# A merge of two instruction streams planned with traced VectorE times and a ScalarE clock, in a kernel of windowed attention and capacity-routed experts

## Chip, cores and metric

The kernel runs on one core of one Trainium2 chip. The metric is the device time of one execution in microseconds (us); of several runs the median counts. The engines are named as the profile names them: PE (TensorE matmuls), PEld (its weight loads), DVE (VectorE), ACT (ScalarE), POOL (GpSimd) and SP (SyncE).

## What is computed

Attention over a window of 64 positions feeds a layer of eight experts. Each token goes to one expert; an expert takes at most 576 tokens, and tokens are handed out in the order of all 4608 x 8 logits. Cut to what matters:

```python
# attention: batch 8, heads 8, seq 576, head_dim 64, causal window 64
x = attn_out.transpose(0, 2, 1, 3).reshape(4608, 512)
logits = x @ w_gate                       # 4608 x 8
order = np.argsort(-logits.flatten())
for idx in order:                         # greedy, cap = 576 tokens for each expert
    tok, e = idx // 8, idx % 8
    if assigned[tok] >= 0 or counts[e] >= cap: continue
    assigned[tok] = e; counts[e] += 1
for e in range(8):
    h = np.maximum(x[assigned == e] @ w1[e], 0.0)     # 512 -> 1024
    out[assigned == e] = h @ w2[e]                    # 1024 -> 512
```

## The kernel before

The attention comes first (to about 149 us); it also leaves the logits in the tile `L` and the rows of x in DRAM (`xs`). After it, three kinds of work run side by side, all on the same five engines.

**Routing** (`Routing.steps(p)`, p = 0 to 7). Pass p finds the p-th expert that fills up, and its 576 tokens. A pass begins with the choices of each token (six DVE operations, L499 to L506, which end with the tile `one`), goes through eight rounds, and ends with the list of the tokens. A round compares the values with 15 thresholds on DVE (tile `G`, L514), counts on PE (nine matmuls, L593, from here on "a count"), and works out the next thresholds in a chain of small DVE operations (L602 to L654). For p of 1 and more, ACT first spreads `one` fourfold (three copies, L557, into `one4`), which the counts read. The list is made by a sum over positions on PE (L707, L708), one-hot tiles on DVE and ACT (`A`, `B`, `R`, L739 to L748), 18 matmuls (L756), a copy `ils` on DVE (L763) and 8 small matmuls (L768), and ends in the tile `idx` (L774).

**Transposes** (`Experts.turn(p, idx)`). POOL gathers the tokens' rows of `xs` in five indirect DMAs (`xg`, `rest`, L957). PE transposes each tile of 128 tokens (4 matmuls, L975; two PSUM tiles `tp`), ACT rounds it to the high part `xh` (L946), DVE subtracts for the low part `xl` (L950). For p of 1 and more the tiles go as two, two and one.

**Products** (`Experts.steps(p, idx)`). The first product takes 192 matmuls (`h`, L1021), whose results ACT and DVE turn into `hh` and `hl` (L993, L998); the second takes 16 (L1054) and 96 (`o`, L1064), whose results ACT copies (`low`, `ot`, L1038, L1035) and POOL stores by an indirect DMA (L1043). The three terms are xh·wh, xh·wl and xl·wh. `Experts.load` fetches the weights on SP's queue (`st`), ACT makes `wh` (L900) and the negative of it (L911), and POOL's accumulating DMA adds `st` to make `wl` (L913).

Every engine executes in the order in which the program is recorded. That order comes from `Streams.run`: each piece of work is a generator that records instructions and yields a delay in ns, and the generators are resumed in the order of a reckoned clock. `busy(dt, eng)` reckons an engine as a queue: it adds dt to the engine's end and returns how far off that is. Before the change DVE work is entered by `dve(dt)`, which puts 0.4 dt on the queue and 0.6 dt behind it; ACT has no queue, its work is a plain delay. `GATHER`, `JOIN` and others are constants of that clock. For p > 1 a group of transposes waits until the routing has recorded its next matmuls (`self.joins > n0`), or until `JOIN` ns have passed:

```python
    def dve(self, dt):
        return self.busy(0.4 * dt, "dve") + 0.6 * dt
...
                n0, t0 = self.joins, self.clock() + JOIN[tiles[0] // 2]
                yield lambda: self.routed or self.joins > n0 or self.clock() >= t0
```

Below, "expert p" is the expert of pass p, and H_p, O_p are its first and second product.

Of the kernel before, what the change touches and what calls it, by code (L numbers as in the profile page):

```python
# [10 lines left out]
FT = mybir.dt.float32  # L11
FR = mybir.dt.float32r
BF = mybir.dt.bfloat16
# [10 lines left out]
E = 8  # L24
# [374 lines left out]
class Routing:  # L399
# [132 lines left out]
    def dve(self, dt):  # L532

        return self.busy(0.4 * dt, "dve") + 0.6 * dt

    def steps(self, p):
# [7 lines left out]
        if p < E - 1:  # L544
# [19 lines left out]
            for r in range(NR):  # L564
# [4 lines left out]
                if not p:  # L569
# [8 lines left out]
                    yield self.dve(1350)  # L578
                else:
                    c4 = self.room(128, 72)  # L580
                    cn, c4 = c4[:, 64:72], c4[0:M, 0:4 * ND]
                    for j0, j1 in ((0, 20), (20, 36)):
                        self.compare(G, thr, j0, j1)
                        yield self.dve(420)
                    for f in rest:
                        f()
                    yield self.dve(200) + slack
# [18 lines left out]
                    yield self.dve(450)  # L606
# [60 lines left out]
                yield self.dve(400)  # L667
            for f in rest:
                f()
            yield self.dve(200)  # L670
# [11 lines left out]
            yield self.dve(600)  # L682
# [8 lines left out]
            yield self.dve(600)  # L691
        else:
# [7 lines left out]
            yield self.dve(800)  # L700
# [4 lines left out]
        yield self.dve(250) + (600 if p else 0)  # L705
# [7 lines left out]
                                       op0=OP.add, op1=OP.mult)  # L713
        si = tile_([128, 3, NJ], I32, name="si")
        nc.vector.scalar_tensor_tensor(si[:, 0], Y[:, 0], -1.0, Y[:, 1], op0=OP.add, op1=OP.add)
        yield self.dve(500)
# [4 lines left out]
        yield self.dve(500)  # L721
# [18 lines left out]
        yield self.dve(410)  # L740
        nc.scalar.activation(Rw[:, 0], pairs(A_), AF.Copy, scale=self.lane)
        if p:
            nc.vector.tensor_tensor(Bw, pairs(self.r32), sb[:, 1].rearrange("p (q h) -> p q h", h=2)[:, None]
                                    .to_broadcast([128, 32, NJ // 2, 2]), OP.is_equal)
            yield self.dve(1200)
        for j0, j1 in ((0, NJ),) if p else ((0, 18), (18, 36)):
# [5 lines left out]
            yield self.dve(600) + slack + (500 if p else 0)  # L752
# [7 lines left out]
            yield self.busy(n * (18 if p else 29) + (90 if p else 0))  # L760
        yield self.dve(200) + slack
        ils = tile_([72, 32, 2], BF, name="ils")
        nc.vector.tensor_copy(ils.rearrange("p a h -> p (a h)"), il[0:72])  # L763
        yield self.dve(300)
# [7 lines left out]
        yield self.busy(100) + 200 + slack  # L772
# [4 lines left out]
        if p < E - 1:  # L777
            if not p:
                nc.vector.scalar_tensor_tensor(self.eid, m, T[:, 0:1], best, op0=OP.is_gt, op1=OP.mult)
            eq = tile_([128, NJ], FT, name="eq")  # L780
            nc.vector.scalar_tensor_tensor(eq, Y[:, 1], CAP + 0.5, X[:, 1], op0=OP.is_lt, op1=OP.mult)
            nc.vector.scalar_tensor_tensor(self.eid, eq, code[:, 0:1], self.eid, op0=OP.mult, op1=OP.add)
            nc.vector.tensor_scalar(self.un, self.eid, 0.0, None, op0=OP.is_equal)
            yield self.dve(400)
            e1 = tile_([128, E], FT, name="e1")
            nc.vector.tensor_scalar(e1, self.cw, code, -FAR, op0=OP.is_equal, op1=OP.mult)
            nc.vector.tensor_tensor(V, V, e1[:, None, :].to_broadcast([128, NJ, E]), OP.add)
            yield self.dve(600)

            nc.vector.scalar_tensor_tensor(self.oh, m[:, :, None].to_broadcast([128, NJ, E]), T[:, 0:1], one,  # L790
                                           op0=OP.is_gt, op1=OP.mult)
            c2 = tile_([128, E], BF, name="c2")
            with nc.allow_low_precision(reason="whole numbers up to 36"):
                nc.vector.tensor_reduce(c2, self.oh.rearrange("p j e -> p e j"), axis=AX.X, op=OP.add)
            e2 = tile_([128, E], FT, name="e2")
            nc.vector.tensor_scalar(e2, self.cw, code, -1.0e6, op0=OP.is_equal, op1=OP.mult)
            nc.vector.tensor_tensor(self.left, self.left, e2, OP.add)
            if 0 < p < E - 2:
                self.kept = c2
                yield self.dve(1100)  # L800
                return
            yield self.dve(1100) + (slack if p < OWN else 1500)
            cn = self.room(128, E)
            nc.tensor.matmul(cn, self.ones, c2, start=True, stop=True)
            self.joined()
            yield self.busy(110) + 200 + slack
            nc.vector.tensor_tensor(self.left, self.left, cn, OP.add)
            yield self.dve(200)
# [21 lines left out]
class Experts:  # L830
# [34 lines left out]
    def load(self, p, ei):  # L865
# [26 lines left out]
        for i in range(2 * NCH):  # L892
# [8 lines left out]
            yield 1050  # L901
# [7 lines left out]
            else:  # L909

                nc.scalar.activation(lo, hi.bitcast(FT), AF.Copy, scale=-1.0)  # L911
                yield 1150
# [25 lines left out]
    def turn(self, p, idx):  # L938
# [4 lines left out]
        def evac(a, n, t):  # L943
# [4 lines left out]
            yield 700  # L948
# [12 lines left out]
        there = self.clock() + self.busy(6400, "pool") + GATHER[p > 0]  # L961
# [4 lines left out]
        for tiles in ((0, 1), (2, 3), (4,)) if p else ((0,), (1,), (2,), (3,), (4,)):  # L966
            yield max(0, there - 1280 * (4 - tiles[-1]) - self.clock())
            if p > 1:

                n0, t0 = self.joins, self.clock() + JOIN[tiles[0] // 2]  # L970
                yield lambda: self.routed or self.joins > n0 or self.clock() >= t0
            for n, a in enumerate(tiles):
# [3 lines left out]
                dt = self.busy(260)  # L976
# [7 lines left out]
    def steps(self, p, idx):  # L984
# [44 lines left out]
        self.first += 1  # L1029

        def put(a, o):
            ot = fw.tile([128, DM], FT, name="ot", bufs=3)
            m = 128 if a < 4 else 64
            if a < 4:
                nc.scalar.activation(ot, o, AF.Copy)  # L1035
            else:
                t = fw.tile([64, DM], FT, name="low")
                nc.scalar.activation(t, o[64:128], AF.Copy)  # L1038
                yield 650
# [67 lines left out]
def body(tc, q, k, v, vt, wg, w1, w2, xs, out):  # L1107
    nc = tc.nc
    with ExitStack() as ctx:
# [17 lines left out]
        def route():  # L1127
            for p in range(E):
                for dt in rt.steps(p):
# [3 lines left out]
                    if p in rt.idx and p not in listed:  # L1133
                        listed.add(p)
                        st.add(ex.turn(p, rt.idx[p]))
                    yield dt
            ex.routed = True
# [6 lines left out]
        known, listed = set(), set()  # L1144
# [20 lines left out]
```

## Time and profile before

| | |
|---|---|
| median of 3 runs | 650.95 us (649.75 to 651.98) |
| profiled execution | 650.87 us, its span 648.9 us |
| PE busy in the span | 611.3 us (94%) |
| DVE, ACT, POOL busy | 454.1, 346.1, 186.2 us |
| mean granted TensorE clock | 0.972 |

The span runs from the first to the last instruction; 1.97 us lie around it. A row of the timeline gives the start, the duration, engine, line, operation, output and inputs with their shapes, how many instructions were merged, and in brackets how long the engine had been idle and what released it. Matmuls are pipelined, so a matmul's duration overlaps the next one's: the pitch of a run of matmuls is read from their starts. PEclk is the granted TensorE clock, 1.00 for 2.4 GHz and 0.50 for 1.2 GHz.

### The profile page before, as it was taken

The page shows a single profiled execution, that of the slowest core. Times are in us where ns is not written, and L with a number is a line of the kernel's source. Part 1 is how long each engine was busy: PE and PEld are TensorE (multiplying, and loading weights), DVE is VectorE, ACT ScalarE, POOL GpSimd, SP SyncE. Part 2 cuts the span into 40 slices and gives each one's busy share as a digit, 9 for nine tenths or more (in the row PEclk, how much of TensorE's full clock was granted, in tenths as well). Part 3 has the DMA queues.
Part 4 walks back from the last instruction along what each step waited for, and adds up shares of the span by engine and source line. Part 5 has one row for each costly group of instructions (what it writes and reads, how often), then busy time and mean ns, then how long its engine had stood idle before and what let it go on. Part 6 is the DMA issues. An engine that isn't in the chain of part 4 may idle for free.

```text
span 648.9 us, 16904 instructions
## 1 busy us (share of the span) xinstructions
PE 611.3 (94%) x6375; PEld 532.0 (82%) x6375; DVE 454.1 (70%) x2126; ACT 346.1 (53%) x724; POOL 186.2 (29%) x242
## 2 busy tenths in 40 slices
PE   8899999994599999999899999999999999999996
PEld 6677778884389879978797898899789879989985
DVE  7788888886789868876786787688678755523300
ACT  6798999980265176337526643572664354524210
POOL 1334353331141162026105411620541164011011
PEclk9999999996599998999899999999999999999999
DMA  9999999931376199459918964991896399411001
GB/s 313 373 367 368 371 385 368 336 109 36 130 237 130 30 315 240 82 195 218 234 21 300 246 120 149 247 242 30 295 248 122 124 273 321 153 36 38 1 25 48
DMA packets 44657, 127.81 MB, mean 197 GB/s; under 512 B 4632, under 2 KB 5272, under 8 KB 44576
## 3 DMA queue, kind: packets, MB, share of 16 engines
q1 hardware_dynamic: 30736, 79.52, 34.1%
q0 software_dynamic: 13552, 46.69, 30.8%
q8 instruction: 50, 0.82, 0.5%
q10 hardware_dynamic: 288, 0.52, 0.3%
q14 instruction: 31, 0.25, 0.1%
HBM read 82.15 MB, written 18.87 MB: 156 GB/s over the span
## 4 chain that ended last, share of the span: by engine, by line
PE 49%; issue 20%; POOL 4%; DMA 2%; ACT 1%; DVE 0%; POOLq 0%; ACTq 0%
PE h L1021 22%; PE o L1064 18%; PE o L1054 3%; POOL out L1043 2%; PE rps L593 2%; DMA wl<-st 1%; PE tp L975 1%; POOL xg L957 1%; DMA xg<-xs,idx 1%; POOL wl L913 1%; PE rps L756 1%; ACT wh L900 0%; ACT wl L911 0%; PE rps L758 0%; POOLq L1161 0%
## 5 line engine op out<-in xcount | busy, mean ns | idle before, releaser
L1043 POOL DMA_INDIRECT out<-ot,idx x40 | 40.4, 1010 | 252.8 <-ACT ot L1035 87.8
L993 ACT ACTIVATE hh<-h 128x256 fp32r<-128x256 f32 (+1 forms) x128 | 52.4, 409 | 110.3 <-PE h L1021 109.0
L1064 PE MATMUL o<-wh,hh 128*128 128x512 f32 x256 | 101.4, 396 | 0.0
L1064 PE MATMUL o<-wh,hl 128*128 128x512 f32 x256 | 100.8, 394 | 0.0
L1064 PE MATMUL o<-wl,hh 128*128 128x512 f32 x256 | 100.5, 393 | 0.0
L141 ACT ACTIVATE pe<-st,mx 128x128 f32<-128x128 f32 x288 | 92.0, 393 | 5.8 <-DVE mx L136 5.5
L1021 PE MATMUL h<-xh,wh 128*128 128x256 f32 (+1 forms) x512 | 93.0, 302 | 1.7 <-issue 0.9
L1021 PE MATMUL h<-xl,wh 128*128 128x256 f32 (+1 forms) x512 | 93.4, 300 | 0.0
L998 DVE SCALAR_TENSOR_TENSOR hl<-h,hh 128x256 fp32r<-128x256 f32 x128 | 53.6, 419 | 56.5 <-ACT hh L993 55.9
L1021 PE MATMUL h<-xh,wl 128*128 128x256 f32 (+1 forms) x512 | 91.9, 299 | 0.0
L1021 PEld LDWEIGHTS h<-xh,wh 128*128 128x128 f32 x512 | 76.8, 192 | 2.8 <-ACT xh L946 1.4
L1021 PEld LDWEIGHTS h<-xh,wl 128*128 128x128 f32 x512 | 76.7, 192 | 0.0
L1021 PEld LDWEIGHTS h<-xl,wh 128*128 128x128 f32 x512 | 76.6, 192 | 0.0
L900 ACT ACTIVATE wh<-st 128x1024 fp32r<-128x1024 f32 x64 | 67.3, 1052 | 2.7 <-DMA st<-w 2.5
L136 DVE CUSTOM_DVE_ANT_0 st<-Sp,mask 128x128 f32<-128x128 f32 x288 | 63.7, 285 | 5.7 <-PE Sp L128 5.2
L913 POOL DMA_DIRECT2D wl<-st x49 | 44.6, 976 | 68.9 <-ACT wl L911 25.9
L1035 ACT ACTIVATE ot<-o 128x512 f32<-128x512 f32 x32 | 19.1, 597 | 70.9 <-PE o L1064 63.2
L1064 PEld LDWEIGHTS o<-wh,hl 128*128 128x128 f32 x256 | 48.1, 188 | 9.6
L1064 PEld LDWEIGHTS o<-wl,hh 128*128 128x128 f32 x256 | 48.1, 188 | 9.3
L1064 PEld LDWEIGHTS o<-wh,hh 128*128 128x128 f32 x256 | 48.1, 188 | 9.3
L911 ACT ACTIVATE wl<-wh 128x1024 fp32r<-128x1024 f32 x49 | 51.8, 1056 | 0.6
L168 PE MATMUL Op<-VO,pt 128*64 128x73 f32 x640 | 45.3, 230 | 2.5 <-ACT pt L150 1.1
(182 smaller groups left out, 1093.2 us busy)
## 6 DMA issues: line engine op xcount, KB each, us to landing
st<-w SPq DMA_DIRECT2D x60, 512.0 KB
wl<-st POOLq DMA_DIRECT2D x49, 512.0 KB
xs<-x SPq DMA_DIRECT2D x36, 256.0 KB
VO<-v SPq DMA_DIRECT2D x6, 1168.0 KB
Q<-q SPq DMA_DIRECT2D x6, 1152.0 KB
K<-k SPq DMA_DIRECT2D x6, 1152.0 KB
VT<-vt SPq DMA_DIRECT2D x6, 1152.0 KB
VO<-v SPq DMA_DIRECT2D x4, 584.0 KB
```

Source lines behind the costliest of these rows:

```text
L136: nc.vector.tensor_tensor_reduce(st[:, h, :], Sp[h % 2][:, h // 2], mk, scale=-0.125, scalar=3.0e38, op0=OP.add, op1=OP.min, accum_out=mx[ ...
L141: nc.scalar.activation(pe[:, h, :], st[:, h, :], AF.Exp, bias=mx[:, h:h + 1], scale=-1.0)
L168: nc.tensor.matmul(Op[64 * a:64 * a + 64, g, h, :], pt[:, h, 64 * a:64 * a + 64], vv[a][:, 4 * g + h, :], start=True, stop=True)
L900: nc.scalar.activation(hi, st[i], AF.Copy)
L911: nc.scalar.activation(lo, hi.bitcast(FT), AF.Copy, scale=-1.0)
L913: nc.gpsimd.dma_start(lo.bitcast(FT), st[i], accum_op=OP.add)
L993: nc.scalar.activation(hh[:, f, c0:c1], h, AF.Relu)
L998: nc.vector.scalar_tensor_tensor(t, h[:, a - c0:b - c0], 0.0, hh[:, f, a:b].bitcast(FT), op0=OP.max, op1=OP.subtract)
L1021: nc.tensor.matmul(h, wv[:, cc, 128 * (f % 2):128 * (f % 2) + 128], xt[:, cc, c0:c1], start=(k == 0), stop=(k == 11))
L1043: nc.gpsimd.indirect_dma_start(out=self.out[5 * p + a], out_offset=IndirectOffsetOnAxis(ap=idx[0:m, a:a + 1], axis=0), in_=ot[0:m], in_off ...
L1054: nc.tensor.matmul(o, hh[:, f, 512:], w[:, 512 * (f % 2):512 * (f % 2) + 512], start=(f == 0 and n == 0), stop=(f == NF - 1 and n == 1))
L1064: nc.tensor.matmul(o, ht[:, f, 128 * a:128 * a + 128], wt[:, 512 * (f % 2):512 * (f % 2) + 512], start=(k == 0), stop=(k == 23))
```

## The change

It changes no instruction's work, only the numbers and rules of the reckoned clock, and so the order in which instructions are recorded. `dve(dt, n)` now holds the queue for all of dt but 110 ns per operation, and most durations get new values. ACT becomes a queue (`busy(dt, "act")` in `load`, `turn`, `evac`, `put`). For p of 1 and more the first comparison no longer waits for the copies of `one` (a fixed 3500 ns before); the counts wait for what is left of the copies' reckoned time. `GATHER` says that gathers land earlier, and `JOIN` gets a second limit, counted from the start of the second product. The list's last part moves into `listing`, which starts the transposes by a call. The lines marked + carry the numbers of the new file.

```diff
-    def dve(self, dt):
-        return self.busy(0.4 * dt, "dve") + 0.6 * dt
+    def dve(self, dt, n=1):
+        return self.busy(dt - 110 * n, "dve") + 110 * n
...
-                yield 3500 if p > 1 else 300
+                copied = self.clock() + self.busy(1260, "act") + 200
...
                         self.compare(G, thr, j0, j1)
-                        yield self.dve(420)
+                        yield self.dve(480 - 4 * j0)
                     for f in rest:
                         f()
-                    yield self.dve(200) + slack
+                    if r:
+                        self.dve(360, 2)
+                    yield max(slack, copied - self.clock() if own and not r else 0)
...
-                    yield self.dve(450)
+                    yield self.dve(530, 2) + (150 if kept is not None else 0)
...
-                    yield self.dve(400)
+                    yield self.dve(490, 2)
...
-                    yield self.dve(400) + slack
+                    yield self.dve(430, 2)
...
-                yield self.dve(400)
+                yield self.dve(450, 2) if r else self.dve(700, 3)
...
+        yield self.dve(260)
+        yield from self.listing(p, Y, slack)
...
+    def listing(self, p, Y, slack):
...
         nc.scalar.activation(Rw[:, 0], pairs(A_), AF.Copy, scale=self.lane)
+        lanes = self.clock() + self.busy(880, "act") + 100
...
-            yield self.dve(600) + slack + (500 if p else 0)
+            yield max(self.dve(810 if p else 740, 1 if p else 2) + slack, lanes - self.clock())
...
-        self.idx[p] = idx
+        self.listed(p, idx)
...
-GATHER = (2900, 6500)
+GATHER = (2900,) + (4200,) * 7
...
-JOIN = (800, 2000, 3300)
+JOIN = ((800, -1800), (2000, 900), (3300, 2000))
+SECOND = 27500
...
             nc.scalar.activation(hi, st[i], AF.Copy)
-            yield 1050
+            yield self.busy(1050, "act")
...
             nc.scalar.activation(xh[:, :, r], t[:, :, :n], AF.Copy)
             self.tiles[p] = a + 1
-            yield 700
+            yield self.busy(520 if n > 64 else 300, "act") + 160
...
-        there = self.clock() + self.busy(6400, "pool") + GATHER[p > 0]
+        there = self.clock() + self.busy(6400, "pool") + GATHER[p]
...
-                n0, t0 = self.joins, self.clock() + JOIN[tiles[0] // 2]
+                n0, (t0, t1) = self.joins, JOIN[tiles[0] // 2]
+                t0 = min(self.clock() + t0, self.started + SECOND + t1)
                 yield lambda: self.routed or self.joins > n0 or self.clock() >= t0
...
-                dt = self.busy(260)
+                dt = self.busy(355)
...
             nc.scalar.activation(hh[:, f, c0:c1], h, AF.Relu)
-            yield 500
+            yield self.busy(310, "act") + 160
...
         self.first += 1
+        self.started = self.clock()
...
+        def listed(p, idx):
+            rt.idx[p] = idx
+            ex.routed = p == E - 1
+            st.add(ex.turn(p, idx))
```

How the order changes at three places:

First, DVE in the round of pass 3 that runs beside the last two full tiles of expert 2 (`xl` is a tile's low part, `hl` one of a product, `num` to `G` the round's chain). Before:

```order
L950 TENSOR_TENSOR xl<-tp,xh 128x4x128
L616 TENSOR_SCALAR pq_504<-cnt 128x8
L618 STREAM_TRANSPOSE pt<-pq_504 128x32
L998 SCALAR_TENSOR_TENSOR hl<-h,hh 128x256
L950 TENSOR_TENSOR xl<-tp,xh 128x4x128
L621 TENSOR_REDUCE ps<-pt 128x1
L623 STREAM_TRANSPOSE num<-ps 128x32
L998 SCALAR_TENSOR_TENSOR hl<-h,hh 128x256
L646 TENSOR_REDUCE d<-num 128x1
L654 SCALAR_TENSOR_TENSOR thr<-tab,d,base 128x15
L514 TENSOR_TENSOR G<-m,thr 128x300
L514 TENSOR_TENSOR G<-m,thr 128x240
```

Now:

```order
L961 TENSOR_TENSOR xl<-tp,xh 128x4x128
L618 TENSOR_SCALAR pq_504<-cnt 128x8
L620 STREAM_TRANSPOSE pt<-pq_504 128x32
L623 TENSOR_REDUCE ps<-pt 128x1
L625 STREAM_TRANSPOSE num<-ps 128x32
L961 TENSOR_TENSOR xl<-tp,xh 128x4x128
L648 TENSOR_REDUCE d<-num 128x1
L656 SCALAR_TENSOR_TENSOR thr<-tab,d,base 128x15
L514 TENSOR_TENSOR G<-m,thr 128x300
L514 TENSOR_TENSOR G<-m,thr 128x240
```

The two `hl` have left the round. On PE this round's counts were 8 transposes and 18 matmuls of H_2 apart; now 8 transposes, the last 5 matmuls of O_1, 12 of H_2, 4 transposes and 9 of H_2 stand between them.

Second, ACT at the end of expert 0's second product, where the tiles of expert 1 are turned (`one` is pass 2's copy, the last `ot` the last tile of O_0). Before:

```order
L1035 ACTIVATE ot<-o 128x512
L900 ACTIVATE wh<-st 128x1024
L911 ACTIVATE wl<-wh 128x1024
L557 COPY one_4885<-one 128x384 x3
L1035 ACTIVATE ot<-o 128x512
L946 ACTIVATE xh<-tp 128x4x128
L900 ACTIVATE wh<-st 128x1024
L946 ACTIVATE xh<-tp 128x4x128
```

Now:

```order
L1048 ACTIVATE ot<-o 128x512
L911 ACTIVATE wh<-st 128x1024
L922 ACTIVATE wl<-wh 128x1024
L911 ACTIVATE wh<-st 128x1024
L922 ACTIVATE wl<-wh 128x1024
L1048 ACTIVATE ot<-o 128x512
L557 COPY one_4905<-one 128x384 x3
L957 ACTIVATE xh<-tp 128x4x128 x2
```

The copies moved behind the last `ot`, which waits for the end of O_0; the conversion between the two `xh` moved ahead. On PE the list of pass 1 (L768) now stands 27 matmuls before the end of O_0 instead of 37.

Third, ACT beside the last list (`R`, pass 7) and the first tiles of expert 6. Before:

```order
L741 ACTIVATE R<-A,lane 128x18x18x2
L900 ACTIVATE wh<-st 128x1024
L1035 ACTIVATE ot<-o 128x512
L911 ACTIVATE wl<-wh 128x1024
L946 ACTIVATE xh<-tp 128x4x128 x4
```

Now:

```order
L782 ACTIVATE R<-A,lane 128x18x18x2
L957 ACTIVATE xh<-tp 128x4x128 x2
L911 ACTIVATE wh<-st 128x1024
L922 ACTIVATE wl<-wh 128x1024
L957 ACTIVATE xh<-tp 128x4x128 x2
```

Two weight conversions and an `ot` no longer stand ahead of the first two `xh`. On PE, 7 matmuls of O_5 instead of 1 now stand between these transposes and the 18 matmuls of the list.

## Rows read from the trace of the kernel before

**Rows 1.** Chain that ended last, in order of time: start us, us, what
```profile
347.87 10.42 PE o L1064 x45
...
366.06 3.23 PE h L1021 x27
...
423.02 3.23 PE h L1021 x27
...
479.95 3.23 PE h L1021 x27
```
**Rows 2.** Timeline, the start of H_2 and pass 3's rounds beside it
```profile
302.69 0.74 PE L1021 MATMUL h<-xh,wh 128*128 128x256 f32 x4 [0.32 <-ACT xh L946]
...
304.95 0.57 PE L593 MATMUL rps<-G,one 128*128 128x60 bf16 x9
...
307.79 0.64 PE L1021 MATMUL h<-xl,wh 128*128 128x256 f32 x4
307.93 0.69 DVE L950 TENSOR_TENSOR xl<-tp,xh 128x512 fp32r<-128x512 f32 x1
...
309.15 0.42 DVE L998 SCALAR_TENSOR_TENSOR hl<-h,hh 128x256 fp32r<-128x256 f32 x1 [0.20 <-ACT hh L993]
...
309.94 0.79 DVE L514 TENSOR_TENSOR G<-m,thr 128x300 bf16<-128x300 f32 x2
...
310.47 0.59 PE L593 MATMUL rps<-G,one 128*128 128x60 bf16 x9 [2.05 <-DVE G L514]
...
311.89 1.14 PE L1021 MATMUL h<-xh,wh 128*128 128x320 f32 x4 [0.47 <-ACT xh L946]
```
**Rows 3.** Windows of 4 us behind two pauses: busy of each engine, PEclk, DMA share, GB/s
```profile
244.00:248.00 4.00, 3.82 (x21) 3.85 (x22) 3.66 (x15) 2.72 (x6) 1.36 (x2) 0.57 1.06 213
312.00:316.00 4.00, 4.00 (x17) 4.00 (x18) 1.84 (x9) 1.58 (x3) 0.00 (x0) 0.57 1.05 289
```
**Rows 4.** Timeline, pass 7's list beside O_5
```profile
531.68 0.39 PE L1064 MATMUL o<-wl,hh 128*128 128x512 f32 x1
...
532.32 0.69 DVE L950 TENSOR_TENSOR xl<-tp,xh 128x512 fp32r<-128x512 f32 x1 [2.08 <-ACT xh L946]
...
532.93 0.21 DVE L763 CAST ils<-rps 72x64 bf16<-72x64 f32 x1
...
533.19 0.23 PE L768 MATMUL rps<-s,ils 72*32 72x5 bf16 x8 [1.12 <-DVE ils L763]
```
**Rows 5.** Timeline, from pass 1's list to the start of H_1
```profile
231.97 0.22 PE L768 MATMUL rps<-s,ils 72*32 72x5 bf16 x8
...
237.27 0.46 DVE L506 TENSOR_TENSOR one<-w,best 128x288 bf16<-128x288 bf16 x1
...
237.94 1.32 ACT L557 COPY one<-one 128x384 bf16<-128x384 bf16 x3
...
240.64 0.79 PE L975 MATMUL tp<-identr,xg 128*128 128x128 f32 x8
...
242.71 0.53 PE L975 MATMUL tp<-identr,xg 128*128 128x128 f32 x4 [0.98 <-DVE xl L950]
...
244.70 1.18 PE L1021 MATMUL h<-xh,wh 128*128 128x256 f32 x4
```
**Rows 6.** Timeline, two rounds of pass 5 beside O_3, H_4 and expert 4's tiles
```profile
415.15 0.42 PE L593 MATMUL rps<-G,one 128*128 128x60 bf16 x9
...
420.55 0.57 PE L593 MATMUL rps<-G,one 128*128 128x60 bf16 x9
...
424.93 0.42 DVE L998 SCALAR_TENSOR_TENSOR hl<-h,hh 128x256 fp32r<-128x256 f32 x1
...
425.27 0.40 DVE L514 TENSOR_TENSOR G<-m,thr 128x240 bf16<-128x240 f32 x1
...
426.09 0.43 PE L593 MATMUL rps<-G,one 128*128 128x60 bf16 x9
```
**Rows 7.** The page, groups: what xcount | busy, mean ns | idle before, releaser
```profile
L900 ACT ACTIVATE wh<-st 128x1024 fp32r<-128x1024 f32 x64 | 67.3, 1052 | 2.7 <-DMA st<-w 2.5
...
L1035 ACT ACTIVATE ot<-o 128x512 f32<-128x512 f32 x32 | 19.1, 597 | 70.9 <-PE o L1064 63.2
```

More of the change, by code (lines that the diff above doesn't have):

```diff
@@ L704, in steps @@
         nc.vector.tensor_tensor_scan(run, Xf, Xf, 0.0, op0=OP.add, op1=OP.bypass)
-        yield self.dve(250) + (600 if p else 0)
+        yield self.dve(340) + slack
         pos = self.room(128, 2 * NJ, not p)
@@ L713, in steps @@
                                        op0=OP.add, op1=OP.mult)
+        yield self.dve(260)
+        yield from self.listing(p, Y, slack)
+        if p < E - 1:
+            if not p:
+                nc.vector.scalar_tensor_tensor(self.eid, m, T[:, 0:1], best, op0=OP.is_gt, op1=OP.mult)
+            eq = tile_([128, NJ], FT, name="eq")
+            nc.vector.scalar_tensor_tensor(eq, Y[:, 1], CAP + 0.5, X[:, 1], op0=OP.is_lt, op1=OP.mult)
+            nc.vector.scalar_tensor_tensor(self.eid, eq, code[:, 0:1], self.eid, op0=OP.mult, op1=OP.add)
+            nc.vector.tensor_scalar(self.un, self.eid, 0.0, None, op0=OP.is_equal)
+            yield self.dve(750, 4 - (p > 0))
+            e1 = tile_([128, E], FT, name="e1")
+            nc.vector.tensor_scalar(e1, self.cw, code, -FAR, op0=OP.is_equal, op1=OP.mult)
+            nc.vector.tensor_tensor(V, V, e1[:, None, :].to_broadcast([128, NJ, E]), OP.add)
+            yield self.dve(730, 2)
+            nc.vector.scalar_tensor_tensor(self.oh, m[:, :, None].to_broadcast([128, NJ, E]), T[:, 0:1], one,
+                                           op0=OP.is_gt, op1=OP.mult)
+            c2 = tile_([128, E], BF, name="c2")
+            with nc.allow_low_precision(reason="whole numbers up to 36"):
+                nc.vector.tensor_reduce(c2, self.oh.rearrange("p j e -> p e j"), axis=AX.X, op=OP.add)
+            e2 = tile_([128, E], FT, name="e2")
+            nc.vector.tensor_scalar(e2, self.cw, code, -1.0e6, op0=OP.is_equal, op1=OP.mult)
+            nc.vector.tensor_tensor(self.left, self.left, e2, OP.add)
+            if 0 < p < E - 2:
+                self.kept = c2
+                yield self.dve(1550, 3)
+                return
+            yield self.dve(1550, 3) + 300
+            cn = self.room(128, E)
+            nc.tensor.matmul(cn, self.ones, c2, start=True, stop=True)
+            self.joined()
+            yield self.busy(110) + 200 + slack
+            nc.vector.tensor_tensor(self.left, self.left, cn, OP.add)
+            yield self.dve(200)
@@ L714, in steps @@
+    def listing(self, p, Y, slack):
+        nc = self.nc
+        tile_ = self.wk.tile
         si = tile_([128, 3, NJ], I32, name="si")
         nc.vector.scalar_tensor_tensor(si[:, 0], Y[:, 0], -1.0, Y[:, 1], op0=OP.add, op1=OP.add)
-        yield self.dve(500)
+        yield self.dve(230)
         nc.vector.tensor_scalar(si[:, 1], si[:, 0], 5, None, op0=OP.arith_shift_right)
@@ L759, in steps @@
             self.joined()
-            yield self.busy(n * (18 if p else 29) + (90 if p else 0))
-        yield self.dve(200) + slack
+            yield self.busy(n * (15 if p else 29) + (90 if p else 0))
+        yield 150 + slack
         ils = tile_([72, 32, 2], BF, name="ils")
         nc.vector.tensor_copy(ils.rearrange("p a h -> p (a h)"), il[0:72])
-        yield self.dve(300)
+        yield self.dve(260) + slack
         ip = self.room(128, 5, not p)
@@ L771, in steps @@
             self.warm(28)
-        yield self.busy(100) + 200 + slack
+        yield self.busy(255) + 200 + slack
         idx = self.rt.tile([128, 5], U32, name=f"idx{p}")
         nc.vector.tensor_copy(idx, ip)
-        self.idx[p] = idx
+        self.listed(p, idx)
         yield self.dve(200)
[L777 to L808, printed above, removed]
     def expert(self, p, code):
@@ L911, in load @@
                 nc.scalar.activation(lo, hi.bitcast(FT), AF.Copy, scale=-1.0)
-                yield 1150
+                yield self.busy(1050, "act") + 100
                 nc.gpsimd.dma_start(lo.bitcast(FT), st[i], accum_op=OP.add)
@@ L1035, in put @@
                 nc.scalar.activation(ot, o, AF.Copy)
+                self.busy(500, "act")
             else:
@@ L1038, in put @@
                 nc.scalar.activation(t, o[64:128], AF.Copy)
-                yield 650
+                yield self.busy(500, "act") + 150
                 self.busy(600, "dve")
@@ L1142, in products @@
                 yield from ex.steps(p, rt.idx[p])
-        known, listed = set(), set()
+        def listed(p, idx):
+            rt.idx[p] = idx
+            ex.routed = p == E - 1
+            st.add(ex.turn(p, idx))
+        known = set()
+        rt.listed, rt.spawn, rt.clock = listed, st.add, ex.clock
         st.add(route())
```

22 lines of the change are left out of this document (9 added, 13 removed).

## The prediction

> **What bounds the kernel now.** First the page: PE is busy for 94% of the span and no other engine for more than 70%, so PE is the resource, and the question is only where it pauses. Then the chain that ended last, whose pieces show the start of each first product: H_3, H_4 and H_5 begin at 366.06, 423.02 and 479.95 [rows 1], 56.96 and 56.93 us apart, with the same pieces each time. A stretch in which PE pauses anywhere would not repeat to 0.03 us, so from about 323 us on PE runs without a pause worth the name, and an order can only lose there. Then the timeline, for what is not like that stretch. H_2 begins at 302.69 [rows 2], 63.4 us before H_3, 6.4 us more than the steady distance. That is where the time is. Last the windows by granted clock: behind the pauses of experts 1 and 2 four microseconds have a mean clock of 0.57 [rows 3], at the lower of the two levels (1.2 GHz) for most of them, while pauses as short as that of the last list [rows 4] are followed by none.
>
> Which wait ends last in the pauses: at expert 2 a count waits 2.05 us for `G`, whose round had two tile subtractions and two `hl` in it, and the transposes of the last tile then make the next product wait 0.47 us for `xh` [rows 2]. At the start of H_2 the wait is for `xh`, 0.32 us. At pass 7's list, PE waits for `ils`, which stands on DVE behind an `xl` that waited 2.08 us for ACT [rows 4]. At expert 1 the second pair of transposes waits for the first pair's `xl` [rows 5].
>
> **The change, part by part.** No instruction is added or removed; the sum is made of pauses that go, and pauses that come. It is made against the profiled execution, 650.87 us, which is the median (650.95) to 0.1 us.
>
> *Expert 2.* The four products that begin at 307.79 end the run of 18; at the pitch of 0.12 us (3.23 us for 27, rows 1) the next would start at 308.27, and the count starts at 310.47: 2.2 us [rows 2]. With the 0.47 us behind the last tile it is 2.7 us. The clock costs 4 x (1 - 0.57) = 1.7 us [rows 3]. In the new order the stretch between these counts holds 5 matmuls of O_1 at 0.23 us (10.42 us for 45, rows 1), 21 of H_2 at 0.12 and 12 transposes, about 5.2 us with the count. The round needs less than that: in pass 5, with two `xl` and one `hl`, `G` ends at 425.67, 5.1 us after the count at 420.55 [rows 6]; without the `hl` (0.34 us by the starts of its neighbours) it is 4.75. So the pause goes, and the drop of the clock with it: 4.4 us gained.
>
> *Start of H_2.* The first pair of tiles is now transposed 23 matmuls before O_1 ends, so `xh` is early: 0.3 us gained.
>
> *Pass 7's list.* 531.68 + 0.23 to 533.19 is a pause of 1.3 us [rows 4]. ACT now does the two `xh` ahead of the weight conversions, and 7 matmuls instead of 1 stand between the transposes and the list's 18. The two `xl` (0.69 each) then end about when PE needs `ils`: I take 1.3 gained here and keep 0.15 for the rest below.
>
> *Expert 1.* PE's place for the list of pass 1 is 10 matmuls (2.3 us) nearer the end of O_0, so O_0 ends 6.35 us after the list, not 8.67 [rows 5]. `one` is ready 5.76 us after the list (237.73 - 231.97). ACT has the last `ot` ahead of the copies: end of O_0 plus 0.15, 0.6 for it [rows 7], 1.32 for the copies, 0.6 for the `xh` (as large as an `ot`), 0.69 for its `xl`: the second pair of transposes begins 9.7 us after the list, its second tile behind the next `xl` at 10.35, and H_1 at 10.8, which is 4.4 us after O_0's end against 4.06 now (240.64 to 244.70). That is 0.35 lost. The next count stands 15 products later (24 before); at the lower clock PE is there at 14.4, while `G`, with the other two `xl` in its round, is ready at 15.0: 0.65 lost. The drop of the clock behind this pause stays.
>
> *The counts beside the tiles of experts 2 to 5.* Count to count was 5.40 us with 8 transposes and 19 matmuls of O_3 [rows 6], and `G` was just ready. Now 18 stand there for experts 2 and 4 (5.17 us): 0.2 us of waiting each. The following round has 17, 4.94 us against the 4.75 reckoned above: none. At expert 5 the second pair is transposed right ahead of a count, so its `xl` open the round: about 5.2 us against 4.9, and a later round is 0.2 us short. With pass 1 and the last list, 0.15 each, this makes 1.1 us. Nearest rows set the ends: nothing, if all rounds need 4.75; 4 us, if ten rounds each miss by 0.4, which is what two more `hl` would cost.
>
> *Gathers, weights, stores.* POOL's gathers of experts 2 to 7 now stand earlier against the products, ahead of stores that used to precede them. I cost this at nothing: the gathers start some 8 us before their transposes; the stores have nobody behind them but their own buffers. The cover that could fail is ACT's, whose conversions wait in order for weights; that is the third rival. SP's queue keeps its order.
>
> Sum: 650.87 - 4.4 - 0.3 - 1.3 + 1.0 + 1.1 = 647.0 us.
>
> On the clock, the rows show that the pause at expert 2, 2.2 us with a count and four transposes before the next 0.47, was followed by the lower level [rows 2, 3]. [...]
>
> **The rivals.** *Expert 1's pause grows.* The copies, an `ot` and two `xh` are now in one line on ACT behind the end of O_0, and the gather has 2.3 us less. For it: PE's room is gone there. Against it: the copies and what follows were added up above and came out at 0.35 us. If ACT is 1.5 us later than that and the lower clock lasts as long again (1.7), the time is 650.2.
>
> *The counts beside the tiles are all too tight.* Ten of them waiting 0.4 us each in place of 0.6 for those at experts 2 to 5 and 0.5 beside: 647.0 + 4.0 - 1.1 = 649.9. For it: `G` and PE met within 0.1 us at 420.55. Against: without `hl` the second rounds have 0.2 us to spare.
>
> *Slower: a conversion holds up the tiles.* In the order of ACT a `wh` stands between the two `xh` of the first pair for experts 2, 3 and 4, and the second `xl` of that pair is in front of `G` on DVE. A `wh` that has to wait for its weights thus holds up `xh`, `xl`, `G`, the count, and with it PE. It decides from about 0.6 us on, the room that the round leaves. At 2 us of waiting, PE stands for 1.4 us and pays 1.7 for the clock, at three experts: 647.0 + 9.3 = 656.3. Against it: ACT waited 2.5 us for weights in 64 conversions all told [rows 7].
>
> *The clock does not come back with the pause:* the lower level behind expert 2 has another cause, or falls elsewhere in that stretch; 647.0 + 1.7 = 648.7.
>
> *No effect:* the pause at expert 2 turns up again at another count, since the round's work stays the same: 650.9. *Better:* no new waits at all, 644.9.
>
> **How the numbers follow.** What a measurement can tell from no change is 0.3%, 2 us: faster is under 649.0, slower over 652.9. Forecast 0.58 (its own range 645.3 to 648.7), expert 1 0.12, tight counts 0.11, held conversions 0.07, clock 0.03, no effect 0.04, better 0.05. The forecast, the better case and the clock count as faster, and about a third to a half of the first two rivals, which reach down to 649: 0.58 + 0.05 + 0.03 + 0.06 = 0.72. Slower are the held conversions and the far end of tight counts, 0.09; the rest, 0.19, is within 0.3%. The range of 644.0 to 650.2 goes from below the better case to expert 1's rival and leaves out the slower cases and little else.
>
> **What would show it.** Right: no wait over 0.5 us before a count in H_2, and a granted clock of 1.00 throughout H_2; H_3 begins about 57 to 58 us after H_2; no wait for `ils` at the last list; O_0's end to H_1 still over 4 us, with half clock behind it; H_3 to H_5 as far apart as before, to half a microsecond. Wrong: counts waiting for `G` at many experts (tight counts), `xh` behind a `wh` that waits for `st` (held conversions), or a second drop of the clock behind expert 1.

## The result, and the profile after

The change takes 646.62 us (median of 9 runs, 644.71 to 648.72), the kernel before 651.98 us in the runs beside them; the ratio is 0.9912, 95% interval 0.9892 to 0.9932, so 4.4 to 7.0 us less. One of the nine runs of the kernel before, at 982 us, is left out of the ratio. The forecast was 647.0 us. The profiled execution took 644.71 us, its span is 643.1 us. The page:

```profile
span 643.1 us, 16893 instructions
...
PE 609.6 (95%) x6375; PEld 530.2 (82%) x6375; DVE 453.9 (71%) x2126; ACT 347.4 (54%) x724; POOL 185.6 (29%) x242
```

The place that carried the forecast is the round of pass 3 beside expert 2's tiles. PE's and DVE's rows from the timeline of the change, which answer to [rows 2]:

```profile
303.53 0.64 PE L1033 MATMUL h<-xh,wh 128*128 128x256 f32 x4
...
304.19 0.65 DVE L961 TENSOR_TENSOR xl<-tp,xh 128x512 fp32r<-128x512 f32 x1
...
305.21 0.79 DVE L514 TENSOR_TENSOR G<-m,thr 128x300 bf16<-128x300 f32 x2
...
306.29 0.28 PE L1033 MATMUL h<-xl,wh 128*128 128x256 f32 x1
306.41 0.43 PE L595 MATMUL rps<-G,one 128*128 128x60 bf16 x9
```

`G` ends at 306.00, the count starts at 306.41 without a wait, 0.12 us after the product ahead of it. No `xh` is waited for at 303.53 either. The windows over that stretch (the columns are those of [rows 3]) have PE busy throughout, at the full clock:

```profile
304.00:308.00 4.00, 4.00 (x43) 3.96 (x42) 3.79 (x16) 3.48 (x7) 1.92 (x2) 1.00 1.01 271
308.00:312.00 4.00, 4.00 (x37) 3.90 (x37) 3.30 (x16) 3.44 (x6) 0.86 (x1) 1.00 1.04 286
312.00:316.00 4.00, 4.00 (x32) 3.95 (x30) 3.65 (x17) 1.93 (x4) 0.86 (x1) 1.00 1.08 236
```

At expert 1 it went the other way. The timeline there, to be read against [rows 5]:

```profile
233.84 0.23 PE L810 MATMUL rps<-s,ils 72*32 72x5 bf16 x8
...
240.47 0.60 ACT L1048 ACTIVATE ot<-o 128x512 f32<-128x512 f32 x1 [0.79 <-PE o L1078]
...
240.97 1.33 ACT L557 COPY one<-one 128x384 bf16<-128x384 bf16 x3
...
242.20 1.09 ACT L957 ACTIVATE xh<-tp 128x512 fp32r<-128x512 f32 x2
...
243.57 0.53 PE L987 MATMUL tp<-identr,xg 128*128 128x128 f32 x4 [0.97 <-DVE xl L961]
...
244.71 0.72 PE L987 MATMUL tp<-identr,xg 128*128 128x128 f32 x4 [0.61 <-PE tp L987]
...
245.23 1.18 PE L1033 MATMUL h<-xh,wh 128*128 128x256 f32 x4
```

The last matmul of O_0 starts at 240.05; ACT does `ot`, the copies and two `xh` one behind the other, the second tile pair waits for `xl`, and H_1 begins 5.18 us after that matmul, 0.89 us later than before (240.41 to 244.70, 4.29 us).

For a balance, each matmul's distance to the next start, less the median distance of its shape over all traces here, is summed by product. That is PE's time over its work, pauses and lower clock together:

| us over the work | H_0 starts | O_0, H_1 | O_1 | H_2 | O_2 to H_5 | O_5 | O_6 | span |
|---|---|---|---|---|---|---|---|---|
| before | 184.02 | 5.27 | 1.25 | 5.73 | 4.03 | 2.68 | 0.17 | 648.9 |
| the change | 184.01 | 5.73 | 0.86 | 0.45 | 4.63 | 1.23 | 0.57 | 643.1 |
| before, once more | 186.18 | 3.93 | 1.25 | 4.18 | 4.07 | 2.63 | 0.15 | 648.1 |
| the change, once more | 187.55 | 6.27 | 0.86 | 0.45 | 4.36 | 2.17 | 0.59 | 647.8 |

With H_0 itself (-0.17) the first two lines differ by 5.84 us, the difference of their spans. Almost all of it is H_2, as forecast, and the last list in O_5. The last two lines are from the experiments: the waits at experts 1 and 2 repeat to 0.2 us, but what H_2 of the kernel before, H_1 and O_5 of the change lost doesn't, and H_0 starts up to 3.5 us later, although the attention ahead of it is the same program. So the spans of the second pair differ by only 0.3 us: PE lost 1.6 us less in the change, and its H_0 started 1.4 us later. One pair of traces doesn't give the size of the change; the medians do.

### The profile page after: what moved, and what is told of

The parts are those of the page before. It is cut to its first block, busy times and chain, and to the rows that moved or that the text cites. A ratio compares the mean times of both kernels' runs of the same rounds, so it can differ in the third digit from the quotient of the medians.

```text
span 643.1 us, 16893 instructions
## 1 busy us (share of the span) xinstructions
PE 609.6 (95%) x6375; PEld 530.2 (82%) x6375; DVE 453.9 (71%) x2126; ACT 347.4 (54%) x724; POOL 185.6 (29%) x242
## 4 chain that ended last, share of the span: by engine, by line
PE 51%; issue 20%; POOL 3%; DMA 2%; DVE 1%; ACT 1%; POOLq 0%; ACTq 0%
PE h L1033 25%; PE o L1078 17%; PE o L1068 4%; PE rps L595 2%; POOL out L1057 2%; DMA out<-ot,idx 2%; PE tp L987 1%; PE rps L521 1%; PE rps L798 1%; POOL wl L924 0%; POOL xg L968 0%; DVE xl L961 0%; POOL rest L968 0%; PE rps L800 0%; ACT one L557 0%
## 5 line engine op out<-in xcount | busy, mean ns | idle before, releaser
L1033 PE MATMUL h<-xl,wh 128*128 128x256 f32 (+1 forms) x512 | 91.7, 298 | 0.0
L968 POOL DMA_INDIRECT xg<-xs,idx x32 | 32.4, 1012 | 71.0 <-DVE eq L722 63.1
```

What stands on the lines that cost most here:

```text
L968: nc.gpsimd.indirect_dma_start(out=g[a][0:n], out_offset=None, in_=self.xs, in_offset=IndirectOffsetOnAxis(ap=idx[0:n, a:a + 1], axis=0))
L1033: nc.tensor.matmul(h, wv[:, cc, 128 * (f % 2):128 * (f % 2) + 128], xt[:, cc, c0:c1], start=(k == 0), stop=(k == 11))
```

## Experiments

Each is the change with the edit shown, unless it says that it starts from the kernel before. The ratio beside a median is to runs of the kernel before on the same chip, with its 95% interval behind it.

**Both kernels once more.**

> The change once more, unaltered, to see which of its pauses repeat. Theory: what the order sets repeats to 0.1 us (no pause before a count in H_2; O_0's end to the first product of H_1 with wl 6.16 us; the transposes behind pass 2's first count 1.1 us late), and what differs is the length of the half clock behind expert 1 (H_1 0.5 to 3 us over its work) and the start of H_0 (183 to 186 us): median 645.5 to 648 us. Rival (the pauses themselves differ from execution to execution): O_0's end to that product differs by over 0.5 us.

> The kernel before once more, unaltered. Theory: the count of pass 3 in H_2 waits for G about 2.2 us again and half clock follows, 4.5 to 5.5 us over the work of H_2; the last list again loses 1.3 us. Rival (that pause was one execution's): H_2 under 1.5 us over its work.

Measured: the change 647.16 us, ratio 0.9937 (0.9908 to 0.9965); the kernel before 650.04 us in one run. The kernel before pauses at the same places by the same amounts:

```profile
308.54 0.64 PE L1021 MATMUL h<-xl,wh 128*128 128x256 f32 x4
311.23 0.59 PE L593 MATMUL rps<-G,one 128*128 128x60 bf16 x9 [2.05 <-DVE G L514]
...
312.64 0.85 PE L1021 MATMUL h<-xh,wh 128*128 128x320 f32 x4 [0.47 <-ACT xh L946]
```

Both waits are those of [rows 2] to 0.01 us. But no lower clock follows, at expert 1 (244 to 248) or here:

```profile
244.00:248.00 4.00, 2.21 (x19) 2.10 (x20) 3.37 (x14) 4.00 (x7) 3.22 (x4) 1.00 1.05 197
308.00:312.00 4.00, 1.95 (x23) 1.66 (x22) 3.44 (x14) 2.82 (x5) 0.87 (x1) 1.00 1.01 298
312.00:316.00 4.00, 3.53 (x25) 3.38 (x25) 2.99 (x14) 2.63 (x4) 0.00 (x0) 1.00 1.06 301
```

So H_2 lost 4.18 us in this execution and 5.73 in the first: 1.55 us is what the lower clock costs there, and it does not come in every execution. Most seem to have it: the mean granted clock of the whole program was 0.972 in the first execution and 0.977 in this one, and of 75 executions of the kernel before beside the experiments 45 had 0.973 or less (median time 651.9 us) and 7 had 0.977 or more (648.7 us). A mean over the program does not say where the clock fell. In the change H_1 began 5.01 us after O_0's end, not 5.18, and the first product with `wl` 5.71, not 6.16: four products at the full clock took 0.70 us there, and 0.98 in the first execution. The waits repeat to 0.2 us, then, not to 0.1, and its H_0 started later (187.55) than expected.

**A pause put back at expert 2, in three sizes.** With n = 2, 4, 6:

```diff
+                    if p == 3 and r == 2:
+                        dum = tile_([128, NJ, E], BF, name="dum")
+                        for _ in range(n):
+                            nc.vector.tensor_tensor(dum, V, V, OP.is_equal)
                     for j0, j1 in ((0, 20), (20, 36)):
```

> The change with two more DVE instructions ahead of the comparison of pass 3's third round, beside expert 2's last tiles (comparisons of 128x288 into a tile that nobody reads, by L500's pitch 0.49 us each): G about 1.0 us later. The count there had 0.4 us to spare. Theory (a pause has to be of some 2 us to be followed by the lower clock): PE pauses 0.6 us, the clock stays at 1.00, span 0.6 us more. Rival (any pause there drops the clock): 0.6 and about 1.7 us more.

> As the kernel with two, with four more DVE instructions, about 2.0 us: PE pauses 1.6 us ahead of that count. Theory (what the prediction took: the pause of 2.2 us at this place in the kernel before cost the pause and 1.7 us of clock): near the border; either 1.6 us, or 1.6 and 1.7. Rival (the lower clock at expert 2 had another cause, such as the transposes in it): the clock stays at 1.00 here and with six.

> As the kernel with two, with six more DVE instructions, about 2.9 us: PE pauses 2.5 us ahead of that count. Theory: some 4 us at a clock of about 0.57 follow, so the stretch from H_2 to H_3 is 2.5 + 1.7 = 4.2 us longer than in the change. Rival (the pause costs only itself): 2.5 us longer, clock 1.00.

Measured over the work of H_2: 0.66, 1.65 and 4.15 us, against 0.45 (the single times, 649.29, 647.98 and 650.54 us, scatter more than that). Two instructions cost 0.2 us, most of them hidden; four cost a pause and no clock; six the pause and more. Each pause was some 0.4 us smaller than expected. The windows with four:

```profile
308.00:312.00 4.00, 3.23 (x31) 3.14 (x31) 3.76 (x17) 2.17 (x5) 0.88 (x1) 1.00 1.07 317
312.00:316.00 4.00, 4.00 (x36) 3.90 (x35) 3.66 (x17) 3.35 (x5) 1.07 (x2) 1.00 1.04 262
```

With six, the timeline of PE at the count, and the windows:

```profile
307.48 0.28 PE L1037 MATMUL h<-xl,wh 128*128 128x256 f32 x1
309.64 0.59 PE L599 MATMUL rps<-G,one 128*128 128x60 bf16 x9 [1.88 <-DVE G L514]
```

```profile
308.00:312.00 4.00, 2.34 (x22) 2.25 (x22) 3.83 (x15) 1.29 (x2) 0.88 (x1) 0.91 1.05 310
312.00:316.00 4.00, 4.00 (x21) 4.00 (x20) 2.24 (x11) 1.95 (x5) 0.86 (x1) 0.66 1.07 264
```

From product to count the gap is 2.16 us with six, 2.04 over the pitch of 0.12; 4.15 - 0.45 - 2.04 leaves 1.66 us for the clock. The mechanism of the forecast, a pause of some 2 us and 1.7 us of clock, is made again by a cause of its own, in the one execution that was traced. The Trainium skill ("TensorE: Matmul & The Clock Gate", section "HAM oscillation — how this bites in real kernels") describes a kernel in which PE waits some 3 to 5 us for a DMA at each step and starts the next step throttled. The pauses here, of 2.0 to 2.2 us, are shorter than those waits, and the lower clock came behind two of the three (means of 0.57 and 0.66 over 4 us) and not behind the one in the second execution of the kernel before.

**Parts of the change.** The set time of the transposes alone, on the kernel before:

```diff
-JOIN = (800, 2000, 3300)
+JOIN = ((800, -1800), (2000, 900), (3300, 2000))
+SECOND = 27500
...
+                n0, (t0, t1) = self.joins, JOIN[tiles[0] // 2]
+                t0 = min(self.clock() + t0, self.started + SECOND + t1)
...
+        self.started = self.clock()
```

> The kernel before with one part of the change alone: the second limit on the transposes (27.5 us from the start of the second product, less 1.8 us for the first pair). Theory (the gain is the order of PE and DVE beside the second and third tile of expert 2): the second pair of transposes stands behind 3 matmuls of H_2 in place of 18, so the long round is split otherwise; the pause of 2.2 us shrinks to under 1 us and the half clock behind it goes, and the pause at the last list (1.3 us) stays: about 647.5 to 649 us, 2 to 3.5 us under the kernel before. Rival (the round's work is what counts, and the new times of DVE and ACT are needed to find its place): the pause turns up again at the neighbouring count, with the half clock, and the time stays within 1 us of the kernel before, 650 to 652 us.

Measured: 648.4 us, ratio 0.9983 (0.9954 to 1.0012); the profiled execution, 645.73 us, was the fastest of ten. H_2 is 0.67 us over its work, so this part alone ends that pause. But O_2 to H_5 lost 6.50 us, not 4.03, since the last tile (`rest`) now comes late at each of experts 3 to 5, as here:

```profile
365.00 0.71 PE L1023 MATMUL h<-xh,wh 128*128 128x320 f32 x3 [0.48 <-ACT xh L947]
```

That gives back 2.5 us: with the old times this limit finds no place that suits the other experts too.

On the last list the theory was wrong. O_5 lost 1.50 us, not 2.68, although nothing of the change's ACT queue is in this kernel. PE's order from the transposes to the list is that of the kernel before, and `ils` again stands behind an `xl`, but PE does not wait for it:

```profile
523.62 0.20 PE L708 MATMUL rps<-run,ones 128*128 128x72 bf16 x1
523.86 0.23 DVE L712 SCALAR_TENSOR_TENSOR Y<-rps,X 128x72 f32<-128x72 f32 x1 [1.14 <-PE rps L708]
...
530.03 0.21 DVE L763 CAST ils<-rps 72x64 bf16<-72x64 f32 x1
...
530.29 0.22 PE L768 MATMUL rps<-s,ils 72*32 72x5 bf16 x8
```

What differs is `Y`, which the one-hot tiles are made from: here it starts 0.24 us after its matmul, in both executions of the kernel before 1.56 to 1.57 us (last section). The pause of 1.3 us there comes with the late `Y`.

Next, the change with a fixed wait for the copies:

```diff
-                copied = self.clock() + self.busy(1260, "act") + 200
+                self.busy(1260, "act")
+                yield 3500 if p > 1 else 300
+                copied = 0
```

> The change without one part: a pass's first comparison waits again until the copies have had 3500 ns, as before. Theory (the gain is made at expert 2 and the last list, and the copies' part only moves lists): pass 2's first count stands behind all 16 transposes of expert 1's full tiles, lists stand 3 to 13 matmuls later; no pause over 1 us at H_2; 646 to 648.5 us. Rival (the lead that the copies' part gives is what spaces the tiles of experts 2 to 5): pauses of 0.5 us and more before the counts at experts 2 to 5 come back, 649 us and more.

Measured: 645.73 us, 0.9942 (0.9902 to 0.9982), H_2 0.62 us, O_2 to H_5 3.81 us. Nothing comes back: this part is worth no time that shows. And the change with ACT's work as plain delays:

```diff
-            yield self.busy(1050, "act")
+            yield 1050
...
-            yield self.busy(520 if n > 64 else 300, "act") + 160
+            yield 700
...
-            yield self.busy(310, "act") + 160
+            yield 500
...
```

> The change with ACT's work as plain delays again (1050, 1150, 700, 500 and 650 ns, no queue), all else of it kept. PE now has the second count of pass 2 three matmuls behind twelve transposes, and the count before it only those 15 instructions earlier. Theory (a count that stands nearer to the one before than a round's 4.75 us costs the difference, and a pause of 2 us and more brings the lower clock): the pause at expert 1 grows by 2 to 3 us, all else as in the change: 648.5 to 650.5 us. Rival (expert 1's pause is set by the tiles, and the count is hidden in it): 646 to 647.5 us as the change.

Measured: 649.91 us, 0.9975 (0.9947 to 1.0004). O_0 and H_1 are 8.95 us over their work, 2.7 to 3.2 more than in the change's two traces, and H_0 1.61 instead of 0.5. The longest wait is not at the count, as the theory had it, but for an `xl` ahead of the last tile's transposes:

```profile
250.09 0.75 PE L987 MATMUL tp<-identr,rest 128*128 128x128 f32 x4 [2.01 <-DVE xl L961]
```

H_2 stays at 0.78. By this one trace ACT's queue earns its time at experts 0 and 1; H_2 does without it.

**Expert 1, three ways that failed.** First the order of ACT:

```diff
             if a < 4:
+                if p == 0 and a == 3:
+                    yield 1500
                 nc.scalar.activation(ot, o, AF.Copy)
```

> The change with one instruction of ACT moved: the last tile of O_0 is copied (ot) behind the copies of one in place of ahead of them, as in the kernel before; PE's order differs only in a count of pass 2 that stands 6 products earlier. Theory (ot ahead of the copies is what makes H_1 later): the copies run while O_0 still runs, the first xh starts about 1.3 us earlier, and H_1 begins 0.9 to 1.3 us earlier against O_0's end; 0.5 to 1 us of it is lost again at the next count, so the time is 0 to 0.8 us under the change's. Rival (the gather's landing or DVE holds the tiles): H_1 no earlier, same time.

Measured: 645.31 us, 0.9927 (0.9900 to 0.9953); H_1 begins 4.12 us after O_0's end, 1.06 us earlier, and O_0 and H_1 are still 6.94 us over their work. PE now waits for something else, four matmuls on:

```profile
243.45 1.18 PE L1033 MATMUL h<-xh,wh 128*128 128x256 f32 x4
245.21 1.01 PE L1033 MATMUL h<-xh,wl 128*128 128x256 f32 x3 [0.58 <-DMA wl<-st]
```

The weights' low part, which POOL adds by DMA behind the gathers, lets PE go on 12.09 us after the list (233.12). Then a version with the tiles ahead of the count, by three delays in the reckoned clock:

```diff
-                    yield max(slack, copied - self.clock() if own and not r else 0)
+                    yield max(slack, copied - self.clock() if own and not r else 0) + (4500 if p == 2 and not r else 0)
...
+            if p == 1 and tiles[0] == 2:
+                yield 3500
...
+                if p == 0 and a == 3:
+                    yield 2500
```

> A version meant to be better: the change with three delays in the reckoned clock for expert 1. ACT does the copies of one before O_0 ends, then the two xh of the first pair, then the last ot; PE does 3 products of H_1 ahead of pass 2's first count, 6 more ahead of the second pair of transposes, and 30 more by the second count. Theory (expert 1's pause is the second pair of transposes waiting for the first pair's xl behind ot and the copies): H_1 begins 2.5 to 3 us earlier against O_0's end, the pause shrinks from 2.8 to under 1.2 us and the half clock behind it (1.3 us) goes: 642.5 to 644.5 us. Rival (the other pauses grow as the lists move by ten matmuls): 645.5 to 647 us, as the change.

```profile
243.57 0.62 PE L1035 MATMUL h<-xh,wh 128*128 128x256 f32 x3 [1.22 <-ACT xh L957]
...
246.59 1.22 PE L1035 MATMUL h<-xh,wl 128*128 128x256 f32 x4 [1.90 <-DMA wl<-st]
```

Measured: 650.13 us, 0.9982 (0.9956 to 1.0007). The list is at 234.50, and PE goes on with `wl` again 12.09 us behind it. The second pair of transposes and the count stand behind the waiting product, and O_0 and H_1 are 8.29 us over their work. Then that first `wl` by DVE, with the late `ot`:

```diff
-        return p == 0 and i < 3 or p * 2 * NCH + i >= (E - 2) * 2 * NCH + NCH
+        return p == 0 and i < 3 or p == 1 and i == 0 or p * 2 * NCH + i >= (E - 2) * 2 * NCH + NCH
```

> A version meant to be better: the change, with the last ot of O_0 behind the copies of one, and with the first wl of expert 1 made by a DVE subtraction (1.23 us as the others of that kind) instead of POOL's accumulating DMA, whose landing PE waited for 0.9 us with ot moved and 2.1 us with the tiles first, 12.1 us after pass 1's list each time. Theory (with that landing gone, the tiles set expert 1's pause): H_1 begins 2.2 to 3 us after O_0's end in place of 5.18 and runs 15 products without waiting for wl; the second count, 27 products on, then waits 2 to 2.5 us for G, since four xl and two hl stand in its round; net 1 to 1.5 us gained: 644.5 to 646 us. Rival (the round of the second count decides, however early H_1 begins): the count comes as long after O_0's end as in the change (8.45 us) or later, the half clock behind it is as long, and the time is that of the change, 646 to 648 us.

```profile
244.07 1.16 PE L987 MATMUL tp<-identr,xg 128*128 128x128 f32 x8 [1.97 <-DMA xg<-xs,idx]
```

Measured: 648.64 us, 0.9966 (0.9939 to 0.9992). Now the gather itself is late: PE starts the transposes 8.06 us after the list (236.01), where the change started them after 6.76. Why it landed later was not settled. Each repair meets the next link of a chain that begins at the list.

**The list earlier.** So the last run moves the start of the chain:

```diff
-        slack = SLACK[p]
+        slack = SLACK[p] - (250 if p == 1 else 0)
```

> The change with pass 1 alone reckoned faster again (250 ns less at each of its waits): its list stands 42 matmuls before the end of O_0 (27 in the change, 37 before), and the first transposes of expert 1 stand 12 matmuls before that end. Theory (expert 1's pause is a chain that starts at pass 1's list: the first tiles 6.8 us and the first use of wl 12.1 us after it in the change's runs, and the place of the list sets what of that is hidden): O_0 ends about 9.7 us after the list, the tiles are hidden, and H_1 waits only for wl, about 2 us; O_0 and H_1 together 3 to 4.5 us over their work, not 5.7 to 6.3; with pauses otherwise as in the change, 1.5 to 2.5 us under it: 644 to 646 us. Rival (the counts of pass 1 in H_0, 27 products apart and not 30 to 33, each wait longer for G): H_0 2 to 3 us over its work, not 0.5, and no gain: 646.5 to 648 us.

Measured: 641.76 us (640.91 to 643.25), 0.9871 (0.9841 to 0.9900): faster than either kernel, and each of its five runs is under the fastest of the change's 17 (644.71). Its timeline, from the first pair of tiles to H_1:

```profile
238.32 1.19 PE L987 MATMUL tp<-identr,xg 128*128 128x128 f32 x8 [0.33 <-DMA xg<-xs,idx]
...
239.71 0.42 PE L595 MATMUL rps<-G,one 128*128 128x60 bf16 x9
...
241.90 0.79 PE L987 MATMUL tp<-identr,xg 128*128 128x128 f32 x8
...
243.06 0.39 PE L1078 MATMUL o<-wh,hl 128*128 128x512 f32 x1
...
243.29 0.64 PE L1033 MATMUL h<-xh,wh 128*128 128x256 f32 x4
...
243.76 0.65 PE L1033 MATMUL h<-xh,wl 128*128 128x256 f32 x4
```

Both pairs are transposed while O_0 still has products, and H_1 follows O_0 at 0.23 us without a wait, for `wl` neither, since the list (230.74) is 13.02 us back. O_0 and H_1 are 2.89 us over their work; with the pause the half clock went. H_0 is 0.68 us over its work, not the 2 to 3 of the rival. The theory held, and the gain was larger than expected, as the wait for `wl` did not come.

## Why the prediction was right

The time, the sign and the carrying mechanism came as forecast: -3.9 us in the sum, -5.84 between the first two profiled executions, -4.3 us between the time of the profiled execution before (650.87) and the median after. That the sum meets the median to 0.4 us is in part luck: the pauses at expert 2 were worth more than reckoned, the last list owes most of its gain in the first pair of traces to something that the order does not set, and expert 1 lost more than reckoned.

- *Expert 2, -4.4.* Measured -5.28 in the first pair of traces (H_2, 5.73 to 0.45) and -3.73 in the second. The pauses of 2.2 and 0.47 us went, and with them a third of 0.42 us, between the matmuls of a later count, that the sum had not listed. The second figure is pauses alone, where the sum had 2.7. The step that was too sure is "the drop of the clock with it": the 1.7 us are the right size (1.55 and 1.66 us measured) but do not fall due in every execution. In so far the rival on the clock was right.
- *Start of H_2, -0.3.* -0.39 in both pairs (O_1).
- *The last list, -1.3.* -1.45 in the first pair, -0.46 in the second. The first figure is right by luck. `Y` was late in the kernel before and not in the change there; in the second pair it was late in both, and 0.46 us is left for the order. The step "`ils` stands behind an `xl`" took a symptom for the cause: with the transposes' limit alone `ils` stands behind an `xl` too, and with `Y` early PE does not wait. The sign "no wait for `ils`" came; but in the change's second trace PE waits 0.71 us for `R` instead.
- *Expert 1, +1.0.* Right in sign and mechanism, small in size at the start of H_1. The second pair was reckoned 9.7 us behind the list and came at 9.73; the next count at 15.0, and came at 14.66. But H_1 came at 11.39, not 10.8: three operations of the count's round (0.62 us) stood on DVE between the first pair's two `xl`, so the second ended at 10.77, where the working had 10.35. The loss by H_1's start is 0.89 us, not 0.35; in the balance +0.46, and +2.34 in the second pair, whose kernel before had no lower clock there. The three traces with a pause put back at expert 2 have the change's order at expert 1, and lost 7.21, 6.96 and 6.69 us there: over all five that is 5.73 to 7.21, against 5.27 and 3.93 in the kernel before, so the term is nearer 2 than 1. What the working did not see is `wl`: PE used it first 12.37 and 11.92 us behind the list in the change and waited for it until 12.09 in two experiments, so earlier tiles alone could not have gained much there.
- *Tight counts, +1.1.* +0.60 and +0.29 (O_2 to H_5): the waits at experts 2 to 5 are fewer than reckoned. One sign was missed by little: H_5 began 57.48 and 57.50 us after H_4, 0.55 and 0.57 more than before, where half a microsecond was allowed.
- *The steady stretch.* That H_3 to H_5 repeat to 0.03 us does not show that PE has no pause there: the pauses at expert 2 repeat to 0.01 us as well. The balance has 4.0 us over the work of O_2 to H_5 before, in pieces of under 0.2 us, so the conclusion held. H_3 begins at 365.90; the piece of the chain at 366.06 starts inside it, which makes the distance from H_2 63.2 us and not 63.4. The sum does not use it.
- *Gathers and stores at nothing.* In neither trace of the change does PE wait for a DMA behind expert 1. O_6 lost 0.4 us more in every kernel with ACT's queue; in the change its second pair of transposes waits 0.28 us there for an `xl` that stands behind a subtraction of 1.23 us on DVE. The sum had no term for it.
- *Slower by held conversions.* It did not come: H_2, H_3 and H_4 are 0.45, 0.42 and 0.43 us over their work, and ACT waited 2.1 us for weights in its 64 conversions.

## What to carry to other kernels

Where the busiest engine pauses in a chain that several engines work on, ask where the chain begins: repairs at its end uncovered one link after another here (ACT, then a DMA, then the gather), and an earlier start took 2.7 to 4.3 us out (ratios of 0.9871 against 0.9912 and 0.9937). A planner's times pay where they separate two pieces of work that would meet on one engine; check after such a change what the new times have made later, here the list of pass 1. And take a second profile of the same kernel before a term is put down to the clock or, as at the last list, to the order.

## What the runs showed of the hardware

The same pause need not have the same price. Behind 2.2 us at expert 2 the granted clock had a mean of 0.57 over four microseconds in one execution and 1.00 in another of the same kernel; the waits agree to 0.01 us. In the five traces with the change's order at expert 1 the clock fell behind the pause there each time, but not by as much: the lower of the means over 244 to 248 and 248 to 252 us was 0.50 to 0.77. What decides it no run here shows.

A result of PE reached DVE either 0.24 us or 1.56 us after the start of its last matmul, at the same instruction of pass 7. In the change's first profile, then in its second:

```profile
511.80 0.20 PE L710 MATMUL rps<-run,ones 128*128 128x72 bf16 x1
...
512.04 0.23 DVE L714 SCALAR_TENSOR_TENSOR Y<-rps,X 128x72 f32<-128x72 f32 x1 [0.65 <-PE rps L709]
```

```profile
515.58 0.20 PE L710 MATMUL rps<-run,ones 128*128 128x72 bf16 x1
...
517.14 0.23 DVE L714 SCALAR_TENSOR_TENSOR Y<-rps,X 128x72 f32<-128x72 f32 x1 [1.98 <-PE rps L710]
```

DVE had been idle, and nothing else is shown that it waited for. The late form (1.51 to 1.58 us) came in six of the 14 traces, both of the kernel before among them, the early one (0.24 us) in the other eight. The chain to the last list begins with this `Y`; in the order of the change O_5 lost 1.23 us with the early form and 2.09 to 2.21 in the four traces with the late one. The cause was not found.

The attention, the same program in all, started its last matmul between 148.7 and 152.3 us in the 14 traces, 3.6 us apart; the nine runs of the change span 4.0 us.
